# Two-stage attention and a soft mixture of experts: the other bit of the head number on the partition halves

## The chip, the cores and the metric

One core of one Trainium2 chip runs the whole program. The metric is the device time of one execution in microseconds (us). TensorE is called PE below, its weight loads PEld, VectorE DVE, ScalarE ACT, GpSimd POOL. SyncE (SP) issues the transfers; its queue is SPq in the views.

## The reference, cut to what matters

Inputs: q, k, v of shape (8, 8, 576, 64), that is batch, head, row, column; p of shape (8, 8, 32, 64); and the experts' phi (512, 32), w1 (8, 512, 1024), w2 (8, 1024, 512). All are float32.

```python
def sm_attn(qq, kk, vv):                      # per batch and head
    s = scale * qq @ kk.T
    a = exp(s - max(s, -1)); a = a / (sum(a, -1) + 1e-09)
    return a @ vv
p_packed = sm_attn(p, k, v)                   # 32 packed rows of a head
x = sm_attn(q, p_packed, p_packed)            # (8, 8, 576, 64), then as (4608, 512)
logits = x @ phi                              # (4608, 32 slots)
d = softmax of logits over the 4608 rows;  c = softmax over the 32 slots
slot_input = d.T @ x                          # four slots for each of eight experts
slot_out[e] = relu(slot_input[e] @ w1[e]) @ w2[e]
out = c @ slot_out                            # (4608, 512)
```

## The kernel before, in words

The attention is cut into eight steps. Step `i` takes two batches (`dd = i // 2`) and four heads (`g = i % 2`), so that two steps make a quarter `dd` of the 4608 rows. Each step has six blocks of 0.59 MB: k, q and v of each of its two batches. SP issues all transfers in one order: p, then k, k, q, q, v, v of step 0, of step 1 and so on, then 33 transfers of expert weights, then the output. All of them land in one ring buffer of 120 KB a partition (`RING`, line 15). `pump` (line 151) issues the next transfer as soon as its place in the ring is free; `release` frees a place after its last reader and calls `pump`.

The text `ORDER` (line 19) is an order written out ahead. The loop at its end (line 818) calls one small function per word, and each engine executes its instructions in just that order. A word such as `s1.2.0@0` is function, step (or quarter), part, and the PSUM bank after the `@`; a letter after a colon is the engine that copies. The functions that matter, in the order of one step:

- `kt` (line 326): four 32x32-block transpositions on DVE that bring k into `kT`.
- `s1` (line 335): first scores p k, on PE in tiles of 64x64, over four PSUM banks; `mx1`, `e1`: row maximum (DVE) and exponential (ACT).
- `ap`, `apc`: nine transpositions of the weights `a1` on PE, and their copies; `m` (line 392): a v, 36 products on PE, the first reader of v.
- `ppa`, `pp`, `pt`, `ptc`, `mp`, `mm`: the packed rows of each head, normalized, transposed, and multiplied by phi.
- `qp` (line 485), `qc`: 18 transpositions of q on PE, and their copies.
- `s2` (line 511): second scores, 36 products on PE, into banks 5 to 7; `mx2`, `sb` (DVE), `e2` (ACT), `z2`, `n2` (POOL): their softmax; `a2p`, `a2c`: nine transpositions of it and their copies.

`m` of a step writes banks 6 and 7, which `s2` of the step before has filled: `m` therefore waits until `sb` of the step before has read them. At the end of a quarter come `lg` (logits), `f1` to `f6`, `fd`, `fl` (the running maximum and sum over rows), `gr`, `rt`, `gt`, `rb`, `gs` and `sa` (the slots' input). After the last quarter, the addition at line 948 begins the experts' part: `layer1a`, `layer2` and the output.

A block of q or v is issued in two transfers: `rows9` (line 191) returns a list of two halves, and `pump` gives each half all 128 partitions and 576 of the block's 1152 elements:

```python
s = src[2 * dd + b2, 4 * g : 4 * g + 4].rearrange("(x m) (r t) d -> m x r (t d)", x=2, t=T)
return [s[0], s[1]]
```

Here head = 2x + m: the high bit x of the head number within its four chooses the partition half (0 to 63 or 64 to 127), the low bit m the half of the free axis. The source of one such transfer is a pattern of 2 x 64 x 576 elements, in runs of 2304 bytes. A block of k is issued whole (`rows18`, line 185): 128 rows in a row, each a run of 4608 bytes.

Of the kernel before, what the change touches and what calls it, by code (L numbers as in the profile page):

```python
# [1083 lines left out]
```

## Time and profile before

| | |
|---|---|
| median of 3 runs | 532.76 us (529.87 to 532.98) |
| the profiled execution | 528.18 us, of which the span from first to last instruction is 526.0 us |
| busy: PE, DVE, ACT, POOL | 198.5, 135.0, 88.1, 51.5 us |
| moved by DMA | 72.27 MB, mean 137 GB/s |
| mean granted clock of TensorE | 0.698 of full speed |

Rows of a timeline are: start, length, engine, line, operation, output and input, count, and in brackets the idle time before and what ended it. Rows of windows are: the stretch, its length, busy time (and instructions) of PE, PEld, DVE, ACT, POOL, then the granted clock of TensorE, the mean busy share of the 16 DMA engines, and GB/s. Rows of waits are: engine, tile and line, who was waited for, then total us, times, longest. A product of float32 stands in the trace as two instructions, a transposition as one; so 36 products are x72.

### The profile page before, as it was taken

The numbers are of one execution on the slowest core, as the hardware profiler recorded it, in microseconds if no ns is written. First come the engines' busy times: TensorE is split into PE (matmuls) and PEld (weight loads), VectorE is DVE, ScalarE is ACT, GpSimd is POOL, SyncE is SP. The second block draws the span as 40 slices with busy tenths as digits, with TensorE's granted clock in tenths as the row PEclk, the third lists the DMA queues.
The fourth block names the chain that finished last, engine by engine and source line by source line (L and its number), as shares of the span: only waits on it lengthen the run. The fifth ranks groups of instructions, "written<-read, shape, count | busy, mean of one in ns | idle before, by whom it ended". The sixth has DMA issues, their size and how long they took to land.

```text
span 526.0 us, 5990 instructions
## 1 busy us (share of the span) xinstructions
PE 198.5 (38%) x2507; PEld 131.6 (25%) x2507; DVE 135.0 (26%) x268; ACT 88.1 (17%) x206; POOL 51.5 (10%) x82
## 2 busy tenths in 40 slices
PE   0430631044005400671071008801900576966750
PEld 0220520033004300561061006601600543311340
DVE  3100300051006100720160045204430275431260
ACT  0030120014002200341031003400310121110270
POOL 7000000021002100400040004000320030000000
PEclk9965675559556855796577556955865677997995
DMA  5113111411131113112311311131115995999497
GB/s 154 51 50 126 52 52 51 125 52 52 50 126 52 51 50 126 52 53 77 99 53 52 117 59 52 52 126 52 52 50 177 372 409 219 411 424 420 179 395 324
DMA packets 22202, 72.27 MB, mean 137 GB/s; under 512 B 3744, under 2 KB 4000, under 8 KB 20256
## 3 DMA queue, kind: packets, MB, share of 16 engines
q1 hardware_dynamic: 21648, 71.83, 36.4%
q8 instruction: 20, 0.33, 0.2%
q10 hardware_dynamic: 528, 0.07, 0.1%
q14 instruction: 6, 0.05, 0.0%
HBM read 62.46 MB, written 9.44 MB: 137 GB/s over the span
## 4 chain that ended last, share of the span: by engine, by line
SPq 47%; DMA 26%; PE 15%; DVE 6%; issue 2%; ACT 1%; ACTq 0%; DVEq 0%
SPq L165 38%; DMA ring<-in_k_dram 10%; SPq L169 9%; DMA ring<-in_moe_w_dram 7%; DMA ring<-in_v_dram 5%; DMA ring<-in_q_dram 4%; PE ps L401 3%; PE ps L863 2%; PE ps L491 1%; PE ps L1044 1%; DVE mx L542 1%; DVE a L550 1%; PE ps L727 1%; PE ps L600 1%; PE ps L343 1%
## 5 line engine op out<-in xcount | busy, mean ns | idle before, releaser
L401 PE MATMUL ps<-ring,a1T 64*64 64x128 f32 x576 | 33.6, 394 | 237.6 <-DVE a L550 154.7
L401 PEld LDWEIGHTS ps<-ring,a1T 64*64 64x64 f32 x576 | 29.1, 209 | 242.2 <-DVE a L550 156.6
L329 DVE STREAM_TRANSPOSE kT<-ring 128x576 f32<-128x576 f32 x32 | 23.2, 756 | 237.9 <-DMA ring<-in_k_dram 237.8
L491 PE MATMUL ps<-ident,ring 128*128 128x128 f32 x144 | 26.7, 334 | 42.1 <-DMA ring<-in_q_dram 41.9
L576 POOL TENSOR_TENSOR zt<-a 128x576 f32<-128x576 f32 x7 | 9.8, 1398 | 329.5 <-ACT a L568 329.5
L568 ACT ACTIVATE a<-a 128x1152 f32<-128x1152 f32 (+2 forms) x9 | 9.4, 1055 | 192.4 <-DVE rz L413 100.3
L491 PEld LDWEIGHTS ps<-ident,ring 128*128 128x128 f32 x144 | 20.3, 173 | 46.4 <-issue 40.7
L297 ACT COPY qT<-ps 128x512 f32<-128x512 f32 (+1 forms) x33 | 15.7, 490 | 52.6 <-PE ps L491 52.5
L915 PE MATMUL ps<-ring,hT 128*32 128x512 f32 x112 | 17.2, 697 | 9.7 <-DMA ring<-in_moe_w_dram 9.7
L591 POOL TENSOR_TENSOR a<-a,zs 128x1152 f32<-128x1152 f32 (+1 forms) x8 | 16.2, 2019 | 42.5 <-DVE z_run L707 32.4
L343 PE MATMUL ps<-kT,pB 64*64 64x512 f32 (+1 forms) x256 | 19.9, 443 | 0.0
L519 PE MATMUL ps<-ppT,qT 128*64 128x64 f32 x576 | 18.7, 223 | 0.6 <-ACT mm L297 0.6
L519 PEld LDWEIGHTS ps<-ppT,qT 128*64 128x64 f32 x576 | 17.6, 138 | 1.1 <-ACT mm L297 0.8
L863 PE MATMUL ps<-ring,xz 128*32 128x512 f32 x128 | 15.8, 650 | 0.4 <-DVE xz L948 0.4
L425 ACT ACTIVATE pt<-ps,rzm 128x64 f32<-128x64 f32 x16 | 4.1, 310 | 68.1 <-PE ps L401 68.1
L430 DVE SCALAR_TENSOR_TENSOR pp<-ps,rzm,pt 128x128 f32<-128x128 f32 x16 | 4.8, 344 | 38.3 <-ACT pt L425 38.3
L379 PE MATMUL ps<-ident,a 128*128 128x128 f32 x72 | 12.7, 319 | 2.1 <-ACT a L362 1.9
L359 DVE TENSOR_REDUCE nm<-ps 128x2 f32<-128x1152 f32 x8 | 10.8, 1356 | 9.8 <-PE ps L343 9.8
L301 DVE COPY qT<-ps 128x512 f32<-128x512 f32 (+1 forms) x15 | 7.6, 524 | 19.9 <-PE ps L491 19.8
L362 ACT ACTIVATE a<-ps,nm 128x576 f32<-128x576 f32 x16 | 11.7, 740 | 3.2 <-DVE nm L359 3.2
L343 PEld LDWEIGHTS ps<-kT,pB 64*64 64x64 f32 x256 | 9.6, 145 | 10.8 <-issue 10.0
L297 ACT COPY a1T<-ps 128x384 f32<-128x384 f32 x24 | 10.6, 485 | 9.5 <-PE ps L379 9.4
(132 smaller groups left out, 285.4 us busy)
## 6 DMA issues: line engine op xcount, KB each, us to landing
ring<-in_moe_w_dram SPq DMA_DIRECT2D x31, 1024.0 KB
ring<-in_k_dram SPq DMA_DIRECT2D x16, 576.0 KB
ring<-in_q_dram SPq DMA_DIRECT2D x32, 288.0 KB
ring<-in_v_dram SPq DMA_DIRECT2D x32, 288.0 KB
out_dram<-ring SPq DMA_DIRECT2D x10, 768.0 KB
ring<-in_moe_w_dram SPq DMA_DIRECT2D x2, 512.0 KB
out_dram<-ring SPq DMA_DIRECT2D x2, 512.0 KB
ring<-in_p_dram SPq DMA_DIRECT2D x1, 512.0 KB
```

The costliest lines, as they stand in the source:

```text
L165: nc.sync.dma_start(out=dst[:, n * w : (n + 1) * w], in_=half)
L169: nc.sync.dma_start(out=dst, in_=src)
L297: nc.scalar.copy(dst, src)
L329: nc.vector.transpose(kT[:, b2, c].rearrange("p (t r h) -> p h t r", t=T, h=2), view(f"k{i}.{b2}").rearrange("p (h t c d) -> p h t c d", h ...
L343: nc.tensor.matmul(psf[64 * b2 : 64 * b2 + 64, 1024 * x + n0 : 1024 * x + n1], pB[rs, dd, b2, g, c].rearrange("p w s -> p (w s)"), kT[rs, ...
L379: nc.tensor.transpose(ps[:, bank, o : o + P], a1[:, t].rearrange("p x r -> p (x r)"), ident)
L401: nc.tensor.matmul(ps[64 * b2 : 64 * b2 + 64, b + x, 0:P].rearrange("p (m d) -> p m d", m=2), a1T[rs, t, b2], view(f"v{i}.{b2}").rearrange ...
L491: nc.tensor.transpose(ps[:, bank, o : o + P], view(f"q{i}.{b2}")[:, P * y : P * y + P], ident)
L519: nc.tensor.matmul(psf[64 * b2 : 64 * b2 + 64, o : o + 2 * NS].rearrange("p (u s) -> p u s", u=2), qT[:, b2, n, 64 * x : 64 * x + 64], col ...
L591: (nc.vector if eng == "v" else nc.gpsimd).tensor_tensor(a, a, z.unsqueeze(3).broadcast_to([P, a.shape[1], a.shape[2], NS]), op=ALU.mult)
L863: nc.tensor.matmul(ps[32 * a : 32 * a + 32, b + nh, :], xzf[:, (4 * e + a) * NSLOT : (4 * e + a + 1) * NSLOT], wv[:, j, nh * 512 : (nh + 1 ...
L915: nc.tensor.matmul(ps[32 * a : 32 * a + 32, SO, :], hTf[:, (NJ * e + j) * NSLOT : (NJ * e + j + 1) * NSLOT], w2v(e, j), start=(e == 0 and ...
```

## The change

The low bit m of the head number within its four and the high bit x change places for k, q and v: head = 2m + x, the low bit now on the partition halves. With that, rows of two neighbouring heads follow each other in memory, and one transfer of a block has the source pattern 128 x 2 x 576: 128 rows, of each two runs of 2304 bytes. k is loaded by the same function. What follows from the new place of the heads:

- p: its four transposed pieces are multiplied on PE by a constant selection matrix `sel` (`px`, new) and copied by DVE (`pc`), in place of six products on POOL and two on DVE with the mask `bm`.
- `s1` works in 16 tiles of 32x32 with 288 columns, 32 products in a step, in place of 8 of 512 and 8 of 64 columns in tiles of 64x64.
- `gt` has four products in place of eight, `gs` two per step in place of four.
- phi is loaded by four transfers on ACT's queue in place of one.
- `ORDER` is another text throughout; two lines of it stand for the rest.

```diff
-mx1.0.2 qp.0.4@6 qc.0.3:a qp.0.5@5 qc.0.4:a qc.0.5:v e1.0.1 e1.0.0
+s1.0.0@0 qp.0.0@7 mx1.0.0 qp.0.1@6 qc.0.0:a qp.0.3@5 qc.0.1:a qp.0.4@7
...
-            if isinstance(src, list):
-                for n, half in enumerate(src):
-                    w = width // len(src)
-                    nc.sync.dma_start(out=dst[:, n * w : (n + 1) * w], in_=half)
-            else:
-                if len(src.shape) == 3:
-                    dst = dst.rearrange("p (a b) -> p a b", a=src.shape[1])
-                nc.sync.dma_start(out=dst, in_=src)
+            shape = src.shape[1:]
+            if len(shape) == 2:
+                dst = dst.rearrange("p (a b) -> p a b", a=shape[0])
...
+            nc.sync.dma_start(out=dst, in_=src)
...
-        s = src[2 * dd + b2, 4 * g : 4 * g + 4].rearrange("(x m) (r t) d -> m x r (t d)", x=2, t=T)
-        return [s[0], s[1]]
+        s = src[2 * dd + b2, 4 * g : 4 * g + 4]
+        return s.rearrange("(m x) (r t) d -> (x r) m (t d)", m=2, t=T)
...
-            loads.append((f"k{i}.{b2}", 2 * T * D, rows18(i, b2)))
+            loads.append((f"k{i}.{b2}", 2 * T * D, rows9(k, i, b2)))
...
-    nc.scalar.dma_start(out=phi_sb, in_=phi.rearrange("(a p) s -> p a s", p=P))
+    for m in range(2):
+        for g in range(NG):
+            nc.scalar.dma_start(
+                out=phi_sb[64 * m : 64 * m + 64, 2 * g : 2 * g + 2],
+                in_=phi[P * (2 * g + m) : P * (2 * g + m + 1)].rearrange("(x d) s -> d x s", x=2),
+            )
...
+    def f_px(dd, j, bank, eng):
+        for m in range(2):
+            nc.tensor.matmul(
+                ps[:, bank, NP * m : NP * m + NP],
+                sel[:, m].rearrange("p x h d -> p (x h d)"),
+                tmp[:, NP * dd : NP * dd + NP],
+                start=True,
+                stop=True,
+            )
+        banks["px", dd] = bank
...
-            kT[:, b2, c].rearrange("p (t r h) -> p h t r", t=T, h=2),
-            view(f"k{i}.{b2}").rearrange("p (h t c d) -> p h t c d", h=2, t=T, c=2)[:, :, :, c],
+            kT[:, b2, :, c].rearrange("p m (t r) -> p m t r", t=T),
+            view(f"k{i}.{b2}").rearrange("p (m t c d) -> p m t c d", m=2, t=T, c=2)[:, :, :, c],
...
-        for n0, n1 in ((0, 512), (512, S)):
-            for c in range(2):
-                for b2 in range(2):
-                    for x in range(2):
-                        rs = slice(64 * x, 64 * x + 64)
-                        nc.tensor.matmul(
-                            psf[64 * b2 : 64 * b2 + 64, 1024 * x + n0 : 1024 * x + n1],
-                            pB[rs, dd, b2, g, c].rearrange("p w s -> p (w s)"),
-                            kT[rs, b2, c, n0:n1],
...
+        for c in range(2):
+            for y in range(4):
+                b2, m = y // 2, 1 - y % 2
+                for z in range(4):
+                    rs = slice(32 * z, 32 * z + 32)
+                    nc.tensor.matmul(
+                        ps[32 * y : 32 * y + 32, z, 0 : 32 * T],
+                        pT[rs, dd, m, b2, g, c],
+                        kT[rs, b2, m, c],
...
         for a in range(4):
-            for b2 in range(2):
-                o = 2 * P + a * NSLOT
-                nc.tensor.matmul(
-                    ps[64 * b2 : 64 * b2 + 64, b, o : o + NSLOT],
-                    rt[:, b2, a].rearrange("p w s -> p (w s)"),
...
+            o = 2 * P + a * NSLOT
+            nc.tensor.matmul(
+                ps[:, b, o : o + NSLOT],
+                rt[:, a].rearrange("p b w s -> p (b w s)"),
...
-            for m in range(2):
-                o = 2 * P + a * NSLOT
-                nc.tensor.matmul(
-                    ps[64 * m : 64 * m + 64, b, o : o + NSLOT],
-                    pps_[(NG * dd + g) % 4][:, x, 0],
-                    rb[:, a, m],
...
+            o = 2 * P + 2 * g * NSLOT
+            nc.tensor.matmul(
+                ps[64 * x : 64 * x + 64, b, o : o + 2 * NSLOT],
+                pps_[(NG * dd + g) % 4][:, x, 0],
+                rb[:, a].rearrange("p m s -> p (m s)"),
```

SP's queue at the start of the program and for steps 0 and 1 (p, then k, q, v), before (-) and now (+); the numbers are partitions x runs x elements, and lines of `pump` are L165 and L169 before, L167 now:

```order
-L169 DMA ring<-in_p_dram 128x16x64
-L169 DMA ring<-in_k_dram 128x1152 x2
-L165 DMA ring<-in_q_dram 128x1x576 x4
-L165 DMA ring<-in_v_dram 128x1x576 x4
-L169 DMA ring<-in_k_dram 128x1152 x2
+L167 DMA ring<-in_p_dram 128x16x64
+L167 DMA ring<-in_k_dram 128x2x576 x2
+L167 DMA ring<-in_q_dram 128x2x576 x2
+L167 DMA ring<-in_v_dram 128x2x576 x2
+L167 DMA ring<-in_k_dram 128x2x576 x2
```

The order of the tensors stays; four transfers of q and of v in a step are now two, of twice the size.

PE before, from the second scores of step 1 (L519) to those of step 2: L600 is `a2p`, L379 `ap`, L491 `qp`, L401 `m`, L443 `pt`, L343 `s1`, L465 `mp`.

```order
L519 MATMUL ps<-ppT_170,qT 64x64 x36
L600 MATMUL ps<-ident,a_0_160 128x128 x9
L379 MATMUL ps<-ident,a_157 128x128 x9
L491 MATMUL ps<-ident,ring 128x128 x8
L401 MATMUL ps<-ring,a1T 64x128 x36
L491 MATMUL ps<-ident,ring 128x128 x10
L443 MATMUL ps<-ident,pp_167 128x128 x2
L343 MATMUL ps<-kT,pB 64x512 x8
L343 MATMUL ps<-kT,pB 64x64 x8
L465 MATMUL ps<-phi_sb,ppT_169 64x32 x4
L519 MATMUL ps<-ppT_169,qT 64x64 x36
```

PE at the same place now: L526 is `s2`, L607 `a2p`, L386 `ap`, L498 `qp`, L408 `m`, L450 `pt`, L355 `s1`, L472 `mp`.

```order
L526 MATMUL ps<-ppT_151,qT 64x64 x36
L607 MATMUL ps<-ident,a_0_141 128x128 x9
L386 MATMUL ps<-ident,a_138 128x128 x9
L498 MATMUL ps<-ident,ring 128x128 x8
L408 MATMUL ps<-ring,a1T 64x128 x36
L498 MATMUL ps<-ident,ring 128x128 x9
L450 MATMUL ps<-ident,pp_148 128x128 x2
L498 MATMUL ps<-ident,ring 128x128
L355 MATMUL ps<-kT,pT 32x288 x32
L472 MATMUL ps<-phi_sb,ppT_150 64x32 x4
L526 MATMUL ps<-ppT_150,qT 64x64 x36
```

The kinds of work and their order are the same; one transposition of q has moved behind `pt`, and `s1` is 32 small products instead of 16.

## Rows read from the trace of the kernel before

**Rows 1.** The page's 40 slices: DMA busy tenths, and GB/s.
```profile
DMA  5113111411131113112311311131115995999497
GB/s 154 51 50 126 52 52 51 125 52 52 50 126 52 51 50 126 52 53 77 99 53 52 117 59 52 52 126 52 52 50 177 372 409 219 411 424 420 179 395 324
```
**Rows 2.** Windows: q and v alone, weights, output.
```profile
141.00:147.00 6.00, 0.00 (x0) 0.00 (x0) 0.00 (x0) 0.00 (x0) 0.00 (x0) 0.50 0.13 51
...
450.00:485.00 35.00, 26.25 (x220) 7.96 (x216) 10.70 (x33) 3.41 (x6) 0.00 (x0) 0.94 1.01 420
500.00:524.00 24.00, 7.53 (x31) 5.14 (x29) 8.58 (x15) 9.18 (x19) 0.00 (x0) 0.74 0.97 392
```
**Rows 3.** The chain that ended last, shares by engine (page).
```profile
SPq 47%; DMA 26%; PE 15%; DVE 6%; issue 2%; ACT 1%; ACTq 0%; DVEq 0%
```
**Rows 4.** Waits of all engines over the span.
```profile
DVE kT L329 <- DMA ring<-in_k_dram: 237.8, 8, 43.6
...
PE ps L401 <- DVE a L550: 154.7, 6, 36.5
...
PE ps L401 <- DMA ring<-in_v_dram: 82.9, 6, 18.1
...
PE ps L915 <- DMA ring<-in_moe_w_dram: 9.7, 9, 1.5
```
**Rows 5.** Timeline, the stretch of work between two waits in steps 0 to 2.
```profile
109.68 1.32 DVE L542 TENSOR_REDUCE mx<-ps 128x36 f32<-128x1152 f32 x1
111.03 1.36 DVE L550 TENSOR_TENSOR a<-ps,mx 128x1152 f32<-128x1152 f32 x1
...
112.44 3.86 PE L401 MATMUL ps<-ring,a1T 64*64 64x128 f32 x72 [28.65 <-DVE a L550]
...
116.08 2.17 PE L343 MATMUL ps<-kT,pB 64*64 64x512 f32 x32
...
118.18 0.44 PE L443 MATMUL ps<-ident,pp 128*128 128x128 f32 x2
...
119.57 0.42 PE L465 MATMUL ps<-phi_sb,ppT 128*64 128x32 f32 x8 [0.96 <-DVE ppT L301]
...
119.83 2.30 PE L519 MATMUL ps<-ppT,qT 128*64 128x64 f32 x72
...
122.06 1.30 PE L600 MATMUL ps<-ident,a 128*128 128x128 f32 x9
...
123.20 1.33 PE L379 MATMUL ps<-ident,a 128*128 128x128 f32 x9
```
**Rows 6.** Timeline, a stretch of work with the end of a quarter.
```profile
217.53 1.84 PE L401 MATMUL ps<-ring,a1T 64*64 64x128 f32 x48
...
219.61 1.53 PE L491 MATMUL ps<-ident,ring 128*128 128x128 f32 x12
...
221.88 1.49 PE L727 MATMUL ps<-a,d 64*32 64x256 f32 x36
...
224.34 0.66 PE L747 MATMUL ps<-rep,rt 128*64 128x32 f32 x16 [0.28 <-DVE rt L301]
```
**Rows 7.** Windows in the stretch of Rows 5: its first product, and after.
```profile
112.40:116.30 3.90, 3.86 (x76) 3.83 (x80) 1.73 (x4) 1.16 (x1) 2.48 (x3) 0.56 0.14 54
116.30:120.00 3.70, 2.74 (x48) 1.52 (x42) 1.97 (x6) 0.89 (x3) 2.81 (x4) 1.00 0.13 51
```
**Rows 8.** Timeline, the start of the program.
```profile
5.51 0.77 DVE L312 STREAM_TRANSPOSE a<-ring 128x256 f32<-128x256 f32 x2 [5.51 <-DMA ring<-in_p_dram]
...
7.42 2.71 DVE L329 STREAM_TRANSPOSE kT<-ring 128x576 f32<-128x576 f32 x4
...
21.53 3.20 PE L343 MATMUL ps<-kT,pB 64*64 64x512 f32 x32
```
**Rows 9.** Timeline, the last quarter: last v, logits of a quarter, last second scores, line 948.
```profile
378.43 1.18 PE L624 MATMUL ps<-a2T,mm 128*32 128x288 f32 x16
...
412.62 3.90 PE L401 MATMUL ps<-ring,a1T 64*64 64x128 f32 x68 [14.41 <-DMA ring<-in_v_dram]
...
418.99 2.32 PE L519 MATMUL ps<-ppT,qT 128*64 128x64 f32 x72
...
443.17 0.29 DVE L948 TENSOR_TENSOR xz<-S_run,ps 128x128 f32<-128x128 f32 x1 [0.82 <-PE ps L775]
```

More of the change, by code (lines that the diff above doesn't have):

```diff
@@ new lines @@
+m.1.1 qc.1.3:a z2.0.0:p kt.2.0 m.1.2 qp.1.2@5 kt.2.3 ppa.1.0
+qp.1.5@4 ppa.1.1 qc.1.2:a qc.1.5:a pp.1.0 pp.1.1 kt.2.2 pt.1.0
+ptc.1.0:a ptc.1.1:a s1.2.0@0 rc.0.0 n2.0.0:p mp.1.0 mx1.2.0 mm.1.0:a
+s2.1.0@5 kt.3.1 e1.2.0 s2.1.1 kt.3.0 e1.2.1 a2p.0.0@4 mx2.1.0
+a2p.0.2@3 a2c.0.0:a a2p.0.1@2 a2c.0.2:a ap.2.0@4 a2c.0.1:a ap.2.1@3 sb.1.0
+apc.2.0:a ap.2.2@2 apc.2.1:a qp.2.1@4 apc.2.2:a qp.2.3@3 qc.2.1:a kt.3.2
+m.2.0@6 e2.1.0 qc.2.3:v m.2.1 kt.3.3 z2.1.0:p m.2.2 rz.2.0
+qp.2.4@5 ppa.2.0 ppa.2.1 pp.2.0 qp.2.0@4 qc.2.4:a pp.2.1 qp.2.5@3
@@ new lines @@
+qc.3.2:a f4.0.0 ptc.3.1:a s1.4.0@0 f5.0.0 n2.2.0:p fd.0.0 rw.0.0
+mp.3.0 mx1.4.0 f6.0.0 mm.3.0:a gr.0.0@6 gz.0.0 e1.4.1 a2p.2.2@5
+kt.5.1 rt.0.0:a a2p.2.0@4 rt.0.1:a a2p.2.1@3 kt.5.3 e1.4.0 gt.0.0
+rb.0.0 s2.3.0@0 a2c.2.2:a kt.5.0 a2c.2.0:a a2c.2.1:a kt.5.2 s2.3.1
+rz.4.0 gs.0.0 mx2.3.0 ap.4.0@5 ap.4.1@4 apc.4.0:a ap.4.2@3 apc.4.1:a
+qp.4.1@5 sa.0.0 apc.4.2:a sb.3.0 m.4.0@6 qc.4.1:a m.4.1 e2.3.0
+m.4.2 qp.4.3@5 ppa.4.0 z2.3.0:p ppa.4.1 pp.4.0 pp.4.1 pt.4.0
+qc.4.3:a qp.4.4@4 ptc.4.1:a qp.4.0@5 qc.4.4:a qp.4.5@3 qp.4.2@2 qc.4.0:a
@@ new lines @@
+qc.4.5:a qc.4.2:a s1.5.0@0 ptc.4.0:a rc.3.0 n2.3.0:p mp.4.0 mx1.5.0
+mm.4.0:a s2.4.0@5 kt.6.0 e1.5.0 s2.4.1 kt.6.2 e1.5.1 kt.6.3
+a2p.3.0@4 mx2.4.0 a2p.3.1@3 a2c.3.0:a a2p.3.2@2 a2c.3.1:a ap.5.0@4 a2c.3.2:a
+ap.5.1@3 sb.4.0 apc.5.0:a ap.5.2@2 apc.5.1:a lg.1.0@4 apc.5.2:a rz.5.0
+e2.4.0 m.5.0@6 f1.1.0 fl.1.0 m.5.1 z2.4.0:p kt.6.1 m.5.2
+f2.1.0 ppa.5.1 qp.5.1@5 f3.1.0 ppa.5.0 qp.5.0@3 qc.5.1:a qp.5.3@2
+qc.5.0:a pp.5.1 f4.1.0 qc.5.3:a pp.5.0 qp.5.4@5 f5.1.0 rc.4.0
+pt.5.0 qp.5.2@3 qp.5.5@2 n2.4.0:p qc.5.4:a fd.1.0 rw.1.0 qc.5.2:a
@@ new lines @@
+mp.6.0 mx1.7.0 mm.6.0:a s2.6.0@5 rc.5.0 e1.7.0 s2.6.1 n2.5.0:p
+e1.7.1 qp.7.3@4 mx2.6.0 ap.7.0@3 qc.7.3:a ap.7.1@2 apc.7.0:a ap.7.2@4
+sb.6.0 apc.7.1:a qp.7.0@3 apc.7.2:a a2p.5.2@2 qc.7.0:a a2p.5.0@4 a2p.5.1@1
+rz.7.0 e2.6.0 m.7.0@6 a2c.5.2:v a2c.5.0:a m.7.1 z2.6.0:p a2c.5.1:a
+m.7.2 lg.2.0@5 ppa.7.0 ppa.7.1 pp.7.0 pp.7.1 pt.7.0 f1.2.0
+qp.7.4@4 ptc.7.0:a fl.2.0 ptc.7.1:a f2.2.0 qp.7.1@3 qc.7.4:a f3.2.0
+qp.7.5@2 qc.7.1:a qp.7.2@4 mp.7.0 qc.7.5:a qc.7.2:a rc.6.0 f4.2.0
+mm.7.0:a s2.7.0@0 f5.2.0 n2.6.0:p fd.2.0 rw.2.0 s2.7.1 late.0.0
@@ L82 @@
+mx2.7.1 sb.7.1 gr.2.0@6 mx2.7.2 f6.2.0 sb.7.2 rt.2.0:a a2p.6.2@4
+rt.2.1:a a2p.6.0@3 gz.2.0 e2.7.3 a2p.6.1@2 gt.2.0 e2.7.4 z2.7.3:v
+a2c.6.2:a rc.7.3 a2c.6.0:a z2.7.4:v a2c.6.1:a n2.7.3:p rc.7.4 n2.7.4:v
+a2p.7.0@5 rb.2.0 a2p.7.1@4 a2c.7.0:a gs.2.0 a2c.7.1:a a2p.7.2@5 sa.2.0
 a2c.7.2:a lg.3.0@7 f1.3.0 fl.3.0 f2.3.0 f3.3.0 f4.3.0 f5.3.0
-rw.3.0 fd.3.0 f6.3.0 gz.3.0 gr.3.0@4 rt.3.1:a rt.3.0:v gt.3.0
+fd.3.0 rw.3.0 gr.3.0@4 f6.3.0 rt.3.1:a rt.3.0:a gz.3.0 gt.3.0
 rb.3.0 gs.3.0
```

164 lines of the change are left out of this document (62 added, 102 removed).

## The prediction

> **What bounds the kernel now.** I read the page's slices first [rows 1]: for the first 30 of 40 the DMA engines are busy one to three tenths of the time and mostly move 50 to 53 GB/s; a jump to about 126 comes once a step, where k is loaded. From slice 31 on the same engines move up to 424. The windows say how little is at work [rows 2]: while only q and v are on their way, 0.13 of 16 engines, that is 2.1 engines, carry 51 GB/s, or 24.5 GB/s for one; the weights use 1.01 of the 16 at 420 GB/s, the output 0.97 at 392. The chain that ended last [rows 3] lies for 47% in SP's queue and 26% in transfers, with PE at 15%. The waits then tell who stands still [rows 4]: DVE 237.8 us for k, PE 82.9 us for v in `m`. PE's 154.7 us for DVE's `sb` are the same wait at second hand: in `ORDER`, `mx2` and `sb` stand behind transpositions of the next k, so `m` waits for `sb`, `sb` for k, and k is queued behind q and v. A step moves 2.36 MB of q and v, which takes 46 us at 51 GB/s; so the attention lasts until the last v is read at 412.6 [rows 9]. Only the experts' part is different: there PE waits 9.7 us for weights in total [rows 4] with all 16 engines busy [rows 2].
>
> **What separates slow from fast transfers** in these rows is the pattern of the source: it begins with a count of 2 (x) for q and v, with 128 rows for weights, and the first sixteen of these have a second count of 2 as well (128x2x1024, in slices 31 and 32 at 372 and 409 GB/s [rows 1]). The changed transfers begin with 128 rows. The Trainium skill (DMA: Bandwidth & Descriptors, section "Why a DMA increments its semaphore by 16 and not by 1") lets the slowest count of the two patterns choose the number of engines, at most 16; that is two engines before and sixteen now, as the 2.1 of the rows agree.
>
> **Part 1, transfers.** The runs of 2304 bytes stay for q and v, so I take the rate of one engine from them: 16 x 24.5 = 392 GB/s, equal to the output's row [rows 2]. For k the runs are halved from 4608 to 2304 bytes; it gets the same 392. A step's 3.54 MB then take 9.0 us, all 28.3 MB 72 us. Bounds: 51 GB/s (nothing gained) and 420. At 392, step i's v lands at about 6 + 9(i + 1) us, and the ring holds 120 KB a partition, 4.4 steps of 27 KB, so the loads run ahead as long as a step's work takes over 9 us. The wait that goes is followed by the work itself: what is late next is PE.
>
> **Part 2, one step of work.** Its price is read where work ran without a wait for data [rows 5 to 7]. On PE: `s2` 2.30, `a2p` 1.30, `ap` 1.33, `pt` 0.44, `mp` 0.42 [rows 5]. `m` took 3.86 just after an idle stretch, at a granted clock of 0.56, near the lower level of 1.2 GHz [rows 5, 7]; after PE has been at work the clock is 1.00 (2.4 GHz), and 48 of its 72 instructions took 1.84 [rows 6], so 72 take 2.8. `qp`: 12 took 1.53 [rows 6], 18 take 2.3. `s1` now has 64 instructions of 288 columns in 16 tiles, which no row shows. Its neighbours: 72 of `s2` in 2.30 are 32 ns each, 36 of `gr` (eight tiles, 256 columns) in 1.49 are 41 ns each [rows 5, 6]. That is 2.0 to 2.6 us against 2.17 now; I take 2.4, nearer to `gr`, whose tiles are nearer in size. Were the 16 tiles to stream fully side by side, each would have 2 x 288 columns to pass where each of the four tiles now has 2 x 576, in 2.17 us [rows 5]: about 1.1, the lower end of the range.
>
> The Trainium skill (TensorEngine Tiling (Array Packing), "Theoretical Speedup" and "Instruction Overhead") promises up to 4x where a side is at most 32, and warns of about 60 cycles for each product. Worked out from that page, an estimate: 64 x 60 cycles at 2.4 GHz are 1.6 us for `s1`. The rows' 32 to 41 ns for an instruction speak for more; with the page's value the sum below would be some 6 us less.
>
> PE's sum is 2.30 + 1.30 + 1.33 + 2.3 + 2.8 + 0.44 + 2.4 + 0.42 = 13.3 us. Stalls: in 116.3 to 120.0 PE was idle for 0.96 of 3.70 us [rows 7], the wait of `mp` for the copies behind `pt` [rows 5]; now one `qp` and `s1` stand in that gap and nine `qp` ahead of `pt`, yet the copies of q share ACT with this chain, so I allow 1.2. **A step: 14.5 us.** Other engines: whole DVE has 135.0 us and ACT 88.1 of busy time over the span, under PE's 198.5, and the order of kinds is unchanged, so neither bounds. `mx2` and `sb` (2.7 us [rows 5]) must end before `m`; ahead of `m` PE has `a2p`, `ap` and eight `qp`, 3.7 us, which hide them. Without that cover a step would be 2.7 longer.
>
> **Part 3, ends of quarters.** Per quarter on PE: `lg` 1.18 [rows 9], `gr` 1.49, `gt` and `gs` 0.66 each before [rows 6] (`gs` taken like `gt`), about 0.35 each with half the products, and some 1.1 for the small products of `f2`, `f4`, `f6`: 4.5, with a little waiting 5.0. Three of them lie before the last `s2`. The halved `gt` and `gs` save 0.6 a quarter, 2 us in all, counted in this.
>
> **Part 4, the start.** p lands at 5.51 [rows 8]. On DVE follow four transpositions of p (0.4 each), four copies `pc` and four `kt` (2.71 together [rows 8]; the copies priced like these): some 7 us, so `s1` starts at 12.3. `px` (eight small products), `sel` on POOL and phi's four transfers on ACT's queue, idle until its first copy, lie beside that. In a flowing stretch it is 8.4 us from the start of `s1` to the end of `ap` (116.08 to 124.53) and 7.4 from the start of `m` to `s2` (112.44 to 119.83) [rows 5]; a cold `s1` took 3.20 instead of 2.17 [rows 8], 1.0 more. First `s2`: 12.3 + 8.4 + 7.4 + 1.0 = 29 us. The new `kt` writes the same elements in another order: nothing, bounds -0.1 to +0.1 a piece on DVE, which has room.
>
> **Part 5, the rest.** From the last `s2` (418.99) to line 948 (443.17) are 24.2 us of chained small work without transfers [rows 9], kept at 24. From there to the end are 526.0 - 443.2 = 82.8 us. That code is unchanged; the ring already limited how many weights lay ready (219 GB/s in slice 33, between 409 and 411 [rows 1]), so arriving earlier finds the same 15 MB loaded: kept.
>
> **The sum:** 29 + 7 x 14.5 + 3 x 5 + 24 + 82.8 = 252.3 of span, and 528.18 - 526.0 = 2.2 around it: 254.5, say **255 us**. It is made against the profiled execution, which lies 0.9% below the median of the runs, inside what I round.
>
> **The rivals.**
> 1. *Longer steps.* If `mx2` and `sb` are not hidden, the loop is 17.2 us: 7 x 2.7 = 19 more, and with a start of 32, quarters of 6 and 26 at the end 284. For it: each stretch of work in the trace shows them in front of `m` [rows 5]; against it: there k was late, here PE has 3.7 us of other work. Above 284 lie other exposed waits of several us a step.
> 2. *Transfers stay the bound.* It decides when the rate falls below 3.54 MB / 14.5 us = 244 GB/s. At half of 392 the qkv blocks take 144 us, the last v lands at 150, and with the 526.0 - 412.6 = 113.4 that follow it now [rows 9] and 2.2 the time is 266. For it: 0.59 MB transfers are smaller than the weights' 1 MB. Against: the output's 0.79 MB pieces reach 392 [rows 2]. The Trainium skill (the same DMA page, "Rules for kernel authors") asks for 1 MiB or more in one DMA for the highest bandwidth; by that rule this rival gains.
> 3. *Nothing is spread:* q and v stay on two engines, 528 us. Against it: the order shows 128x2x576 with 128 rows first.
> 4. *The other side, slower:* the count of 2 in the middle (m) sets the engines, and now k falls to two as well. All 28.3 MB at 51 GB/s take 555 us; plus 6 at the start, 113.4 and 2.2, it is 677. It decides if a pattern with 128 rows and then 2 runs is not spread; the weights' 128x2x1024 at 372 to 409 GB/s speak against it.
> 5. *Shorter:* `s1` at 1.1 us and no stalls makes a step 12.0: 237.
>
> **How the numbers follow.** The forecast with its bounds has 0.77; longer than 284 by rival 1 0.10; rival 2 0.06 (mostly inside the range); rival 5 below 238 0.04; rival 3 0.01; rival 4 0.02. The range is 238 (no stalls, `s1` at 1.6) to 284 (rival 1). A measurement of this kernel can tell about 1% from no change. Faster 0.97, same 0.01, slower 0.02.
>
> **What would show it.** In the profile after: DMA near full share with about 390 GB/s in the first slices, then idle while the ring is full; PE's waits for k, q and v near zero; PE busy nine tenths with the clock at 1.00 through the attention; `s2` to `s2` 14 to 15 us, 19 to 20 with a quarter's end; `s1` 2.0 to 2.6 us; line 948 near 169 us. Wrong would be: `m` still waiting for `sb`, ACT as the engine waited for, or an experts' part that is longer than 83 us.

## The result, and the profile after

The changed kernel takes **236.16 us** (median of 4 runs, 234.4 to 238.63) where the kernel before takes 532.48 beside it: a ratio of **0.4428, 95% interval 0.438 to 0.4477**. The forecast was 255 with a range of 238 to 284, so the direction and the main reason held and the size did not: the time lies just under the range. The profiled execution took 237.79 us, 236.0 of them span.

The page's slices for the kernel after: busy tenths of PE, the granted clock of TensorE, busy tenths of DMA, and GB/s (for [rows 1]), and the shares of the chain that ended last (for [rows 3]).

```profile
PE   0987989999799995999997577899959655989000
PEclk9999999999999997799999675579995996599755
DMA  7999999999999999922919000099999998019997
GB/s 161 383 392 391 390 391 390 390 387 391 391 392 388 405 406 403 406 90 60 417 62 350 13 0 0 3 330 431 422 418 422 422 422 332 6 59 409 416 416 301
...
PE 46%; DMA 17%; DVE 17%; ACT 8%; issue 2%; POOL 1%; POOLq 1%; ACTq 0%; DVEq 0%; SPq 0%
```

A slice is now 5.9 us, against 13.2 before. From the second slice on the transfers of q, k and v, and behind them the first weights, run at about 390 GB/s; after slice 17 the DMA engines are idle again and again, while the ring is full. SP's queue, 47% of the chain before, is at 0%. PE leads the chain.

PE's waits over the span, longest groups (engine, line, releaser: us in total, times, longest), for [rows 4]:

```profile
PE ps L920 <- DMA ring<-in_moe_w_dram: 9.4, 9, 1.4
...
PE ps L706 <- DVE z_run L714: 2.8, 1, 2.8
PE ps L450 <- DVE pp L437: 2.2, 4, 1.1
```

No wait of PE for q, k or v is left, and none of `m` for `sb`. What PE waits for in the attention, once it has p, are steps of other engines' work. From the first `s2` to the last it stands idle for 7.5 us in all.

Windows of the kernel after (from:to, us, busy time of PE, PEld, DVE, ACT, POOL with the number of instructions, granted clock, DMA share of 16 engines, GB/s), for [rows 2, 7]: the stretch with full transfers, the start, two periods from `s2` to `s2`, the second end of a quarter, 2.60 us of it by themselves, and the experts' part.

```profile
6.00:94.00 88.00, 78.76 (x1570) 60.43 (x1571) 63.96 (x115) 51.23 (x130) 27.61 (x32) 0.98 1.05 393
11.70:23.50 11.80, 9.38 (x238) 6.90 (x239) 8.24 (x16) 6.63 (x16) 0.00 (x0) 1.00 1.05 391
35.50:48.20 12.70, 12.06 (x262) 9.44 (x258) 9.74 (x15) 8.33 (x21) 5.29 (x7) 1.00 1.05 390
66.50:78.40 11.90, 11.41 (x254) 8.82 (x254) 6.16 (x14) 6.86 (x16) 4.28 (x6) 1.00 1.05 391
78.40:102.30 23.90, 20.52 (x352) 14.82 (x348) 17.82 (x34) 13.52 (x37) 6.58 (x7) 0.86 0.98 388
93.00:95.60 2.60, 2.60 (x71) 1.07 (x72) 0.39 (x2) 0.00 (x0) 0.00 (x0) 0.50 1.04 416
...
150.50:236.00 85.50, 55.77 (x369) 21.48 (x369) 28.93 (x63) 17.14 (x33) 0.00 (x0) 0.78 0.82 332
```

In the two periods PE is busy for 12.06 of 12.70 and 11.41 of 11.90 us, 95 and 96%, where in the second window of [rows 7] it stood idle a quarter of the time. At a quarter's end the granted clock falls: 0.86 over the whole period, and 0.50 in the 2.60 us that begin at 93.00, where PE had just stood idle.

The timeline of PE through the first of these two, from one `s2` to the next (start, us, line; in brackets the idle time ahead), for [rows 5]:

```profile
35.52 2.30 PE L526 MATMUL ps<-ppT,qT 128*64 128x64 f32 x72
37.75 0.55 PE L607 MATMUL ps<-ident,a 128*128 128x128 f32 x3
38.49 0.88 PE L607 MATMUL ps<-ident,a 128*128 128x128 f32 x6 [0.20 <-ACT a L369]
39.21 1.33 PE L386 MATMUL ps<-ident,a 128*128 128x128 f32 x9
40.38 1.09 PE L498 MATMUL ps<-ident,ring 128*128 128x128 f32 x8
41.40 2.20 PE L408 MATMUL ps<-ring,a1T 64*64 64x128 f32 x72
43.52 1.20 PE L498 MATMUL ps<-ident,ring 128*128 128x128 f32 x9
45.16 0.59 PE L450 MATMUL ps<-ident,pp 128*128 128x128 f32 x2 [0.44 <-DVE pp L437]
45.59 0.27 PE L498 MATMUL ps<-ident,ring 128*128 128x128 f32 x1
45.79 2.28 PE L355 MATMUL ps<-kT,pT 32*32 32x288 f32 x64
48.00 0.42 PE L472 MATMUL ps<-phi_sb,ppT 128*64 128x32 f32 x8
48.25 2.30 PE L526 MATMUL ps<-ppT,qT 128*64 128x64 f32 x72
```

Read two columns against each other here: a row's start plus its duration lies past the next row's start. `s2` at 35.52 with 2.30 ends at 37.82, and `a2p` begins at 37.75. The durations of the eleven rows ahead of the next `s2` add up to 13.11 us, PE's busy time in the window is 12.06, and the step is 12.73 long. The sum of durations is thus about a microsecond more than PE's busy time, and the rest of the step is 0.64 us of idle time.

The same timeline at the start, for [rows 8]:

```profile
11.74 1.60 PE L355 MATMUL ps<-kT,pT 32*32 32x288 f32 x64
13.27 2.26 PE L498 MATMUL ps<-ident,ring 128*128 128x128 f32 x18
16.55 1.20 PE L386 MATMUL ps<-ident,a 128*128 128x128 f32 x9 [1.02 <-ACT a L369]
18.05 2.19 PE L408 MATMUL ps<-ring,a1T 64*64 64x128 f32 x72 [0.29 <-ACT a1T L291]
...
23.50 2.30 PE L526 MATMUL ps<-ppT,qT 128*64 128x64 f32 x72
```

The later `s2` begin at 35.52, 48.25, 66.51, 78.42, 102.31, 112.74 and 124.62. Two of the seven periods, 18.3 and 23.9 us, hold the `gr` and `gt` of a quarter's end. The other five are 12.0, 12.7, 11.9, 10.4 and 11.9 us, but only the second, shown above, has each kind of a step's work just once and nothing else: the first, third and fourth of them have no `a2p` (the two long periods have two each), and the last has no `s1` but holds `lg`, `f2` and `f4` of the third quarter. A step of work is thus 12.7 us here, and not the mean of the five, 11.8. Line 948 of the kernel before is line 953 now and stands at 150.49, for [rows 9].

### The profile page after: what moved, and what is told of

Its sections match the earlier page's. It is cut to its first block, busy times and chain, and to the rows that moved or that the text cites. A ratio compares the mean times of both kernels' runs of the same rounds, so it can differ in the third digit from the quotient of the medians.

```text
span 236.0 us, 6352 instructions
## 1 busy us (share of the span) xinstructions
PE 182.5 (77%) x2715; PEld 117.0 (50%) x2715; DVE 126.1 (53%) x248; ACT 92.8 (39%) x228; POOL 47.4 (20%) x76
## 4 chain that ended last, share of the span: by engine, by line
PE 46%; DMA 17%; DVE 17%; ACT 8%; issue 2%; POOL 1%; POOLq 1%; ACTq 0%; DVEq 0%; SPq 0%
DMA ring<-in_moe_w_dram 15%; PE ps L355 6%; PE ps L408 5%; PE ps L868 4%; PE ps L498 4%; PE ps L526 4%; PE ps L1049 3%; PE ps L734 3%; PE ps L607 3%; DVE rw L701 3%; PE ps L386 3%; DVE kT L341 2%; ACT a L369 2%; DMA ring<-in_p_dram 2%; DVE a L557 2%
## 5 line engine op out<-in xcount | busy, mean ns | idle before, releaser
L498 PE MATMUL ps<-ident,ring 128*128 128x128 f32 x144 | 20.4, 279 | 0.0
L526 PE MATMUL ps<-ppT,qT 128*64 128x64 f32 x576 | 18.5, 223 | 0.3 <-ACT mm L291 0.3
L598 POOL TENSOR_TENSOR a<-a,zs 128x1152 f32<-128x1152 f32 (+1 forms) x8 | 16.2, 2020 | 12.3 <-DVE zs L594 10.6
L291 ACT COPY qT<-ps 128x512 f32<-128x512 f32 (+1 forms) x43 | 17.9, 477 | 1.7 <-PE ps L498 1.3
L408 PE MATMUL ps<-ring,a1T 64*64 64x128 f32 x576 | 18.2, 272 | 0.3 <-ACT a1T L291 0.3
L291 ACT CAST cT<-ps 128x512 fp32r<-128x512 f32 x6 | 3.5, 586 | 37.1 <-PE ps L946 37.1
L526 PEld LDWEIGHTS ps<-ppT,qT 128*64 128x64 f32 x576 | 17.5, 138 | 0.7 <-ACT mm L291 0.4
L408 PEld LDWEIGHTS ps<-ring,a1T 64*64 64x64 f32 x576 | 15.8, 133 | 2.7 <-DVE rz L421 0.8
L498 PEld LDWEIGHTS ps<-ident,ring 128*128 128x128 f32 x144 | 15.7, 141 | 2.5 <-issue 1.3
L355 PE MATMUL ps<-kT,pT 32*32 32x288 f32 x512 | 16.4, 446 | 0.7 <-issue 0.4
L549 DVE TENSOR_REDUCE mx<-ps 128x36 f32<-128x1152 f32 (+1 forms) x9 | 12.8, 1421 | 4.5 <-PE ps L526 3.4
L369 ACT ACTIVATE a<-ps,nm 128x576 f32<-128x576 f32 x16 | 11.8, 743 | 6.7 <-DVE nm L366 6.7
L607 PE MATMUL ps<-ident,a 128*128 128x128 f32 x72 | 11.9, 303 | 2.8 <-POOL a L598 1.4
L291 ACT COPY a2T<-ps 128x384 f32<-128x384 f32 x23 | 10.0, 484 | 4.0 <-PE ps L607 4.0
L586 POOL TENSOR_TENSOR zt<-zt 128x288 f32<-128x288 f32 (+2 forms) x21 | 11.2, 535 | 1.6
## 6 DMA issues: line engine op xcount, KB each, us to landing
ring<-in_k_dram SPq DMA_DIRECT2D x16, 576.0 KB, 11.9
ring<-in_q_dram SPq DMA_DIRECT2D x16, 576.0 KB, 11.9
```

Of the source, the lines that this page charges most:

```text
L291: nc.scalar.copy(dst, src)
L355: nc.tensor.matmul(ps[32 * y : 32 * y + 32, z, 0 : 32 * T], pT[rs, dd, m, b2, g, c], kT[rs, b2, m, c], start=(c == 0), stop=(c == 1),)
L369: nc.scalar.activation(a1[:, :, x].rearrange("p t (h r) -> p h t r", h=2), s1v[:, x].rearrange("p h (t r) -> p h t r", t=T), AF.Exp, bias= ...
L408: nc.tensor.matmul(ps[64 * b2 : 64 * b2 + 64, b + x, 0:P].rearrange("p (m d) -> p m d", m=2), a1T[rs, t, b2], view(f"v{i}.{b2}").rearrange ...
L498: nc.tensor.transpose(ps[:, bank, o : o + P], view(f"q{i}.{b2}")[:, P * y : P * y + P], ident)
L526: nc.tensor.matmul(psf[64 * b2 : 64 * b2 + 64, o : o + 2 * NS].rearrange("p (u s) -> p u s", u=2), qT[:, b2, n, 64 * x : 64 * x + 64], col ...
```

## The experiments

The theory: nearly all the gain comes from the transfers' sources, which begin with 128 rows; the rest of the difference to the forecast lies in the price of a step. The rivals: the other edits (tiles, order, gate sums) carry a part of the gain; the larger number of engines is owed to the size or number of the transfers.

### The kernel after once more

The unedited kernel ran beside the first three edits, on the same chip.

> The changed kernel unedited, as the control for the three beside it. Every theory expects 234 to 239 us and the addition after the last quarter near 150 us of the span.

237.3 us (ratio 0.4452, 0.4425 to 0.4478), with line 953 at 150.59. It repeats the result within the intervals.

### Transfers alone undone

Only q's and v's sources go back to two counts, as two transfers for each block; k's stays as changed.

```diff
+        if src is not k:
+            s = s.rearrange("(x m) (r t) d -> m x r (t d)", x=2, t=T)
+            return [s[0], s[1]]
```

> The changed kernel with q and v loaded as before, in two transfers of a block whose source begins with a count of 2 (heads 1 and 2 of each four change places in q and v, so the result is another); k stays in 128 rows. Theory 'the transfers are nearly all of the gain': 51 GB/s and 0.13 of the DMA engines between the bursts of k, 500 to 535 us. Rival 'the new order and the 16 tiles carry a good part': 400 to 480 us.

534.67 us. The window of [rows 2] while q and v alone are on their way, in this kernel:

```profile
141.00:147.00 6.00, 0.00 (x0) 0.00 (x0) 0.00 (x0) 0.00 (x0) 0.00 (x0) 0.50 0.13 50
```

2.1 engines carry 50 GB/s again and no engine computes. Over the span, PE stands 70.1 us for v and 37.7 for q, and DVE 234.5 for k behind them. So everything else in the change, with those transfers left as they were, gains nothing.

### Transfers alone done

The other way round: the kernel before, with one statement edited, so that q and v come as in the changed kernel and the rest is as before.

```diff
-        s = src[2 * dd + b2, 4 * g : 4 * g + 4].rearrange("(x m) (r t) d -> m x r (t d)", x=2, t=T)
-        return [s[0], s[1]]
+        s = src[2 * dd + b2, 4 * g : 4 * g + 4]
+        return s.rearrange("(m x) (r t) d -> (x r) m (t d)", m=2, t=T)
```

> The kernel before with one edit: q and v come in transfers of 128 rows in order (heads 1 and 2 of each four change places in q and v, so the result is another). Theory 'transfers are nearly all': 238 to 250 us, the old first scores 8 x 0.6 = 5 us dearer than now and the rest from an order made for late data. Rival 'the order written for late data keeps k ahead of m and its stretches of 17 us': 260 to 285 us.

237.96 us (0.4491, 0.4463 to 0.4519). A window over the transfers of this kernel:

```profile
6.00:94.00 88.00, 75.31 (x1350) 56.93 (x1358) 64.28 (x121) 46.35 (x114) 31.19 (x36) 1.00 1.02 388
```

All 16 engines at 388 GB/s, with `s1` still in four tiles and the old order. This one edit takes 532 to 238; the new order, the 16 tiles and the gate sums together bring some 1 to 3 us more, which the runs hardly tell from nothing. The kernel of the next experiment, which differs from the changed one in transfer size only, stands beside it on the same chip at 0.4431 (0.4406 to 0.4456), and these two intervals just fail to touch; those of the changed kernel itself (0.438 to 0.4477, and 0.4425 to 0.4478) overlap with this one.

### Transfers of half the size

```diff
-            nc.sync.dma_start(out=dst, in_=src)
+            if key[0] in "kqv":
+                for n in range(2):
+                    nc.sync.dma_start(out=dst[:, n], in_=src[:, n])
+            else:
+                nc.sync.dma_start(out=dst, in_=src)
```

> The changed kernel with each block of q, k and v in two transfers of 0.29 MB, each 128 rows with one run of 2304 bytes. Theory 'the pattern's first count sets the rate, size does not': 375 to 395 GB/s in the first 90 us, the time within 2 us of the changed kernel. Rival 'small transfers cost': 200 to 300 GB/s and 5 to 30 us more.

235.66 us (0.4431). The window over the transfers:

```profile
6.00:94.00 88.00, 79.19 (x1601) 61.12 (x1602) 64.28 (x115) 51.37 (x130) 27.52 (x32) 0.98 1.05 392
```

Transfers of 0.29 MB, queued one behind the other, move 392 GB/s like those of 0.59 MB. Neither number nor size of the transfers is the reason: q's and v's are in number and size those of the kernel before, and only the pattern of their source differs. The Trainium skill (DMA: Bandwidth & Descriptors, "Rules for kernel authors") asks for 1 MiB in one DMA for the highest bandwidth, which was rival 2's support; between 0.59 and 0.29 MB these rows show no loss. The weights' transfers of 1 MB, which also have longer runs, move 420 [rows 2], 7% more, and no run here separates size from run.

### First scores in four tiles

Order, transfers and elements stay; `s1` runs as 32 instructions in four 64 by 64 tiles.

```diff
...
-                    rs = slice(32 * z, 32 * z + 32)
...
+                        rs = slice(64 * x, 64 * x + 64)
...
+                            ps[64 * b2 : 64 * b2 + 64, 2 * x + n, 0 : 32 * T],
+                            pT[rs, dd, 0, b2, g].rearrange("p c s -> p (c s)"),
+                            kT[rs, b2, n, c],
```

> First scores in 16 products of 288 columns in tiles of 64x64 in place of 32 in tiles of 32x32; it multiplies the wrong halves of p and k, so the first scores are not the reference's. Theory 'PE bounds a step': s1 takes 2.1 to 2.2 us instead of 1.6, a step 0.5 longer, the time 239 to 242 us. Rival 'the chain through ACT and DVE bounds a step and s1 lies beside it': s1 is as long, the time within 1 us of the control.

239.38 us (0.4484, 0.4457 to 0.4511) beside 237.3 (0.4452, 0.4425 to 0.4478): 2 us more, at the lower end of what was expected, and the intervals overlap: not told apart. In the profiles line 953 comes 3.6 us later (154.23 against 150.59). A flowing `s1`:

```profile
47.43 2.17 PE L355 MATMUL ps<-kT,pT 64*64 64x288 f32 x32
```

2.17 us, as long as the old `s1` in [rows 5], against 1.60 in 16 tiles. So the 16 tiles shorten an uninterrupted `s1` by a quarter. What that is worth in the whole, up to 8 x 0.57 = 4.6 us, is not shown. Of the 3.6 us between the two profiles 2.1 come from one period, in which the granted clock over `s1` was 0.50 here (4.12 us) and 0.86 in the control (1.79). The four periods from the first `s2` to the fifth are 54.8 us here and 55.6 in the control, which has a gap for issue in them (0.84 us) and this kernel none.

### First scores in twice as many instructions

The same 16 tiles and columns, cut into 128 instructions of 144 columns. It ran twice.

```diff
+        for n in range(2):
+            ns = slice(16 * T * n, 16 * T * (n + 1))
...
-                        ps[32 * y : 32 * y + 32, z, 0 : 32 * T],
+                            ps[32 * y : 32 * y + 32, z, ns],
-                        kT[rs, b2, m, c],
+                            kT[rs, b2, m, c, ns],
```

> The same first scores in 64 products of 144 columns instead of 32 of 288, columns in sum unchanged. Theory 'instructions bound s1, 25 ns each': 128 instructions take 3.1 to 3.3 us, the time 8 to 13 us above the control. Rival 'columns bound it': s1 stays at 1.6 to 1.8 us and the time within 2 us.

255.34 us (0.4771, 0.4744 to 0.4798), 18 us above its companion. Its profiled execution had a granted clock of 0.6 to 0.7 nearly throughout, so its rows price nothing, and it was run again for a profile:

> The kernel of s1_144 once more, for a profile at the usual clock: the first profile had a granted clock of 0.6 to 0.7 throughout, while the timed runs had 0.87 to 0.90 and 252 to 256 us. Theory 'instructions bound s1': at clock 1.00 s1 takes 3.1 to 3.6 us in all eight steps, which is 8 x 1.5 to 2.0 = 12 to 16 us. Rival 'the columns bound it and the clock is lower whenever this kernel runs': s1 takes 1.6 to 1.8 us wherever the clock is 1.00, and other products are longer.

255.07 us, one run, at a clock of 0.876. Rows of its timeline, and of PE's waits:

```profile
44.47 1.97 PE L528 MATMUL ps<-ppT,qT 128*64 128x64 f32 x31 [3.29 <-issue]
...
70.92 2.01 PE L357 MATMUL ps<-kT,pT 32*32 32x144 f32 x128
```

```profile
PE ps L528 <- issue: 6.0, 2, 3.3
PE ps L357 <- issue: 3.0, 3, 1.3
...
PE ps L736 <- issue: 2.1, 1, 2.1
```

Two things come apart. An instruction of half the columns takes 2.01 us / 128 = 16 ns against 1.60 / 64 = 25 ns, so the doubled number costs 0.4 us a step, or 3 in all, and neither expectation for `s1` held. The other loss is new: PE waits 11.1 us in these three groups for nothing that the profile shows, in `s2` and `gr` too, which are not edited. The two together are some 14 of the 17 to 18 us. In all six gaps the DMA engines are full (shares of 1.02 to 1.06). The page counts 25 packets on the queue that loads instructions, against 21 in the kernel after, and the trace has the times of these packets. Each of the six gaps ends 1.3 to 1.5 us after one of them has landed: the longest at 44.47, after a packet that landed at 42.96, the next at 97.23, after 95.82. The one such gap of the kernel after, ahead of `s1` at 34.63, follows a packet at 33.23. From 18 to 76 us the packets land 6.2 to 7.8 us apart. So PE waited there for its instructions, as far as times can show it; whether the full DMA engines delay the packets was not separated by a run.

### First scores with half the columns

64 instructions of 144 columns; the other half of the scores is left at the zeros written once.

```diff
+    nc.vector.memset(psf, 0.0)
...
-                        ps[32 * y : 32 * y + 32, z, 0 : 32 * T],
+                        ps[32 * y : 32 * y + 32, z, 0 : 16 * T],
-                        kT[rs, b2, m, c],
+                        kT[rs, b2, m, c, 0 : 16 * T],
```

> First scores of 144 of the 288 columns only, with 32 products as in the changed kernel; the other columns are left out and hold what the banks held. Theory 'instructions bound s1, 25 ns each': s1 stays at 1.5 to 1.6 us. Rival 'columns bound it': 0.8 to 1.0 us, and the time falls by up to 5 us.

236.74 us, one run. From its timeline:

```profile
35.40 0.73 PE L356 MATMUL ps<-kT,pT 32*32 32x144 f32 x14 [1.54 <-issue]
...
61.14 1.12 PE L356 MATMUL ps<-kT,pT 32*32 32x144 f32 x64
```

`s1` falls to 1.12 us, which is the price of rival 5, and in this one run the kernel gains nothing that shows: line 954, the edited kernel's 953, stands at 149.44, 1.05 us earlier than in the kernel after, where 8 x 0.48 = 3.8 us of PE's work are gone. A part returns as waits for issue in `s1`, 1.7 us against 0.4 (the 1.54 at 35.40 ends 1.5 us after an instruction packet landed), and its first `s1` begins 0.54 us later. With 144 columns at 1.12 and 288 at 1.60, one instruction of the 64 costs 17.5 and 25 ns. A straight line through these two, an estimate, is 7.5 ns for 144 columns and 10 that do not depend on them; the 16 ns of the 128 instructions above lie a little lower.

### Gate sums in eight products again

`gt` as before the change, in two halves of 64 columns: eight products, 16 instructions in the trace, in place of four products, eight instructions.

```diff
+            for b2 in range(2):
...
-                ps[:, b, o : o + NSLOT],
-                rt[:, a].rearrange("p b w s -> p (b w s)"),
...
+                    ps[64 * b2 : 64 * b2 + 64, b, o : o + NSLOT],
+                    rt[:, a, b2].rearrange("p w s -> p (w s)"),
```

> Only gt undone: eight products of 64 columns instead of four of 128. Theory 'half the products do not make gt shorter, since loading 128 columns takes what the products save': gt 0.66 us instead of 0.98 at the full clock, the time 0 to 3 us below the changed kernel. Rival 'halving gained what was predicted': gt longer by 0.3 us each, the time 0 to 2 us above.

238.24 us (0.4465, 0.4438 to 0.4492), beside 235.66 (0.4431, 0.4406 to 0.4456) for the kernel with halved transfers: not told apart. Of `gt`, the kernel after has the first row here and this kernel the second; each is the first end of a quarter.

```profile
65.61 0.98 PE L753 MATMUL ps<-rep,rt 128*128 128x32 f32 x8
```

```profile
66.65 0.66 PE L754 MATMUL ps<-rep,rt 128*64 128x32 f32 x16
```

Eight instructions with a 128-wide tile take longer than sixteen with a 64-wide one, yet the kernel with sixteen is no faster. Its profile has a gap for issue of 1.56 us at 116.68, which ends 1.6 us after an instruction packet landed and has no like in the two profiles of the kernel after.

### The gate's scaling on ACT

In the kernel after, the 128x32 product `rw` was held on DVE. The timeline of DVE, POOL and PE around the second end of a quarter and after the last `s2`:

```profile
90.20 2.12 POOL L598 TENSOR_TENSOR a<-a,zs 128x1152 f32<-128x1152 f32 x1 [0.77 <-DVE zs L594]
90.32 2.04 DVE L701 TENSOR_SCALAR rw<-rep,zg 128x32 f32<-128x32 f32 x1
...
92.51 0.60 PE L706 MATMUL ps<-rw,ones 128*128 128x32 f32 x2 [2.79 <-DVE z_run L714]
93.04 2.59 PE L355 MATMUL ps<-kT,pT 32*32 32x288 f32 x64
...
95.56 2.60 PE L734 MATMUL ps<-a,d 64*32 64x256 f32 x36
...
125.96 3.45 DVE L701 TENSOR_SCALAR rw<-rep,zg 128x32 f32<-128x32 f32 x1
...
143.54 0.20 DVE L701 TENSOR_SCALAR rw<-rep,zg 128x32 f32<-128x32 f32 x1
```

`rw` takes 0.20 us alone and 2.04 while POOL multiplies; it ends when POOL does, at 92.3. PE idles 2.79 us for it (the profile names `z_run`, DVE's next instruction), and then `s1` and `gr` run at half the clock: 2.59 and 2.60 us, against 1.60 and 1.49. POOL beside the `rw` of 3.45 us, which ends at 129.41:

```profile
124.57 2.13 POOL L598 TENSOR_TENSOR a<-a,zs 128x1152 f32<-128x1152 f32 x1 [1.69 <-PE ps L665]
126.64 0.98 POOL L806 MEMSET xz<- 128x1056 f32 x1
127.56 1.83 POOL L808 MEMSET hT<- 128x2080 f32 x1
```

The Trainium skill (SBUF — State Buffer, "Terms") has GpSimd and DVE share a pair of ports under a lock that one of them holds for a full instruction while the other stands; the 2.04 beside 0.20 agrees. The 3.45 outlasted the multiplication and went on through two memsets, so there `rw` stood for more than one instruction. The edit takes `rw` to ACT:

```diff
-        nc.vector.tensor_scalar_mul(rw, rep[:, 0], zg)
+        nc.scalar.mul(rw, rep[:, 0], zg)
```

> The small product rw (line 701, 128x32) is made by ACT instead of DVE. Theory 'DVE's rw is held up while POOL works on SBUF': rw takes about 0.2 us at every quarter's end instead of up to 3.45, PE's 2.8 us wait near 90 us goes, the time falls by 3 to 7 us, to 229 to 233. Rival 'rw is long because its input comes late, or what follows waits for POOL anyway': the time within 1.5 us of the control.

**230.82 us** (0.4352, 0.4329 to 0.4375), 6.5 under its companion's 237.3, with line 953 at 146.08, 4.5 earlier. Its timeline and the window of the same quarter's end, from `s2` to `s2`:

```profile
90.69 0.41 PE L706 MATMUL ps<-rw,ones 128*128 128x32 f32 x2 [0.69 <-ACT rw L701]
91.02 1.60 PE L355 MATMUL ps<-kT,pT 32*32 32x288 f32 x64
93.00 1.49 PE L734 MATMUL ps<-a,d 64*32 64x256 f32 x36 [0.38 <-DVE z_run L715]
```

```profile
78.70:98.60 19.90, 18.29 (x353) 14.11 (x349) 17.66 (x33) 13.76 (x38) 5.86 (x7) 1.00 1.02 403
```

The period shrinks from 23.9 to 19.9 us and the clock stays at 1.00 (2.4 GHz). A wait of 2.8 us cost 4 here. In the control's profile, where the clock fell less after the same wait (`s1` 1.79 us), the period is 23.0, and the cost 3.1.

Both edits together, and the ACT edit once more beside them on one chip:

> rw on ACT and gt in eight products of 64 columns together. If both edits save what their profiles show, gt 0.3 us a quarter and 0.8 at the end, the time is 228 to 231 us, 0 to 2 below rw on ACT alone. Rival: gt is off the path, the same as rw on ACT alone.

> rw on ACT alone once more, beside the kernel with both edits on one chip: 229 to 233 us.

232.87 us with both (0.4383, 0.436 to 0.4406) and **230.54** with `rw` alone (0.4335, 0.4313 to 0.4357). The ACT edit repeats its gain; `gt` in eight products adds none, and is here 1% slower. In the profiles it shortens the two long periods by 0.3 and 0.1 us, but the last period is 1.8 longer, with a gap for issue of 1.53 us at 112.76, the like of the one above. The kernel with `rw` on ACT is the fastest of the study, ahead of both the kernel before and the one after.

## Why the prediction was wrong

The sum, term by term, from the profiled execution:

| term | predicted | measured |
|---|---|---|
| start to first `s2` | 29 | 23.5 |
| seven periods, ends of quarters included | 116.5 | 101.1 |
| last `s2` to line 948 (now 953) | 24 | 25.9 |
| from there to the end | 82.8 | 85.5 |
| around the span | 2.2 | 1.8 |
| sum | 254.5 | 237.8 |

**The bound and the mechanism were right.** The rate was worked out as 392 GB/s and is 393, the shares went from 0.13 to 1.05, and PE waits for none of the three. Undoing the sources alone gives the old time, and doing them alone nearly all of the new one, so this is shown from both sides. By the rule of the Trainium skill that the prediction named (DMA: Bandwidth & Descriptors, "Why a DMA increments its semaphore by 16 and not by 1"), the slowest count of the two patterns, here the source's, limits the number of engines; the shares agree: 0.13 of 16 with a count of 2 in front, and 1.02 to 1.05 with 128. Rivals 2, 3 and 4 are out: the rate is not half of 392, q and v are spread, and k, with its count of 2 in the middle, is too.

**The step that failed is "A step: 14.5 us"**, added seven times: with the ends of quarters 116.5 us, where the loop from the first `s2` to the last took 101.1. The loop's window, and the durations of PE's rows in it added up by kind, beside the prediction's terms:

```profile
23.50:124.62 101.12, 93.62 (x1880) 71.92 (x1876) 68.82 (x127) 62.21 (x159) 35.62 (x42) 0.97 0.89 337
```

| part of the loop | predicted | measured |
|---|---|---|
| rows of steps, end to end | 7 x 13.3 = 93.1 | 87.5 |
| rows of the ends of quarters, end to end | 3 x 4.5 = 13.5 | 14.2 |
| overlap of the rows | 0 | -8.1 |
| PE idle | 7 x 1.2 + 3 x 0.5 = 9.9 | 7.5 |
| sum | 116.5 | 101.1 |

- *The rows were added as if they stood end to end.* This is the largest part, 8.1 of 15.4 us: the durations add up to 101.7, and PE's busy time is 93.6. On the step shown above the prediction's 13.3 and the measured 13.11 nearly agree, but the rows overlap by 1.0. This could have been read before: in [rows 5], `m` at 112.44 with 3.86 ends at 116.30 and `s1` begins at 116.08, and likewise at `s2`, `a2p` and `ap`.
- *One `s1` and one `a2p` were counted twice.* The seven periods hold six of each, not seven. The `s1` of steps 0 and 1 lie before the first `s2` and were priced in Part 4; two `a2p` lie behind the last `s2`, as in the kernel before, and were in the 24 us of Part 5. By the prediction's prices that is 2.4 + 1.3 = 3.7 us.
- *`m` at 2.8 is 2.3 on the mean*, 3.5 us over the loop. It was scaled from 48 instructions. The other way, `qp` at 2.3 is 2.6 and `pt` at 0.44 is 0.54, 2.8 us together.
- *The stalls were put at 1.2 a step.* The step shown has 0.64, of which 0.44 ahead of `pt` is for DVE's `pp`; the 0.96 of [rows 7] for the copies behind `pt` is gone. Of the loop's 7.5 us of idle time 3.6 are waits behind `rw`, so the steps have less than half of the 8.4 given to them.
- *`s1` at 2.4.* It takes 1.60 where nothing interrupts it (three of eight), and over all eight, from first start to last end, with the gaps for issue or ACT's copies and one at half the clock, 2.1 on the mean. The neighbour chosen, `gr`, misled a little: 1.2 us for the six of the loop. But the price of `s1` was not what decided: halving its columns moved the time of one run by nothing that can be told. The prediction's sentence from the Trainium skill (TensorEngine Tiling (Array Packing), "Instruction Overhead") gave 1.6 for it, which is the uninterrupted row, by chance; its 60 cycles, 25 ns, do not bind, since 128 instructions ran at 16 ns each.

**Part 3's count failed too.** "Three of them lie before the last `s2`": two do whole. Of the third only `lg`, `f2` and `f4` do; its `gr` runs after the last `s2`, as it did in the kernel before, and was thus already in the 24 us of Part 5. That the rows of two and a part came to 14.2 us, near the 13.5 for three, is luck: `gt` with "half the products" was not 0.35 but 0.98 and 1.08 in the loop (up to 1.92 after it), and the `gr` at half the clock took 2.60. The wait of `rw` behind POOL no term of the prediction held; moving `rw` gave 4.0 us back in the second end of a quarter.

**Part 4 failed by 5.5 us**, on the same kind of step. `s1` began at 11.74, as worked out (12.3). "8.4 us from the start of `s1` to the end of `ap`" was read in a flowing stretch, where `s2` and `a2p` (3.6 us) stand in between; the start has none, and from `s1` to `m` it took 6.3. The "7.4 from the start of `m` to `s2`" held `m` at 3.86 with the clock at 0.56; with 2.19 it took 5.45. And `s1` was not cold: PE had worked on the small products of `px` up to then, the clock was 1.00, and it took 1.60.

**Part 5 held within 2 and 3 us.** After the last `s2`, `rw` stands 3.45 us behind POOL; moving it gave 0.7 and 1.8 us back there in the two runs with `rw` on ACT (25.2 and 24.1 from the last `s2` to line 953). In the experts' part PE waits as long for weights as before (9.4 against 9.7 us), but at a granted clock of 0.78 it is busy for 55.8 us, where the kernel before had 51.6 at 0.85; why the clock is lower there was not tried.

**The rivals.** Rival 1 fell: no wait of `m` for `sb`. Rival 5 named 237, but by an `s1` of 1.1 and no stalls, and neither is so; its number came near by luck, from the overlap, `m` and the double count. The range ended 2 us too high for the same reason: its lower end was built from the two uncertain terms, stalls and `s1`, and had no room for an error common to all rows. Its ends are also not the sums of the terms named with them: no stalls and `s1` at 1.6 give 254.5 - 7 x 2.0 = 240.5, not 238, and rival 1's terms give 254.5 + 18.9 + 3 + 3 + 2 = 281.4, not 284.
